# Attention's values in halves of TensorE's columns, in plain float32, in a kernel of attention and MLP

## The chip, the cores and the metric

The kernel runs on one core of a Trainium2 chip. The metric is the device time of one execution in microseconds; a run's time is compared as the median of several executions. The profile is one profiled execution of the same program.

TensorE (PE) multiplies; its weight loads (PEld) are listed apart. VectorE (DVE), ScalarE (ACT) and GpSimd (POOL) work on tiles, and SyncE (SP) issues the loads and stores.

## What is computed

Eight sequences of 576 positions go through banded causal attention with 8 heads of 64, and the result through an MLP with a rational function between its two matrices:

```python
scores = scale * q @ k.T            # per head, scale = 1/8
mask = (rel >= 0) & (rel < 128)     # rel = query position - key position
attn = softmax(where(mask, scores - slope[h] * abs(rel), -1e9))
x = (attn @ v)                      # heads side by side: 4608 x 512
h = x @ w_in                        # 512 x 2048
g = (a0 + a1*h + a2*h**2 + a3*h**3) / (1 + |b0|*|h| + |b1|*h**2 + 1e-6)
out = g @ w_out                     # 2048 x 512
```

All of it is float32.

## The kernel before

**Blocks, tiles and stages.** The 4608 positions are 36 blocks of 128. With a band of 128 a block of queries needs two blocks of keys: its own, below the diagonal, and the one before, above it. The MLP goes through 17 tiles: the first and the last of 3 blocks (384 columns), the others of 2. A unit of attention is a tile of one or two blocks of queries for one pair of heads (4 pairs, 128 rows: 64 of each head). `TILES` lists the units' blocks, `MLP` the tiles' blocks. While the MLP runs on tile t, attention prepares tile t + 1, and in the first stage (t = 0) the weights are converted from 64-bit numbers as well; in the next they are split into high and low parts.

**Number formats.** In the first stage all matmuls take plain float32. In the later ones an operand is split into a high part in the format fp32r (a copy by ScalarE) and the low rest (a subtraction by VectorE), and a product is three matmuls: high x high, low x high, high x low. So `x_hi`, `x_lo`, `wi_hi`, `w_lo`, `g_h`, `g_l` come in twos, as do keys and queries (`kq_hi`, `kq_lo`).

**A unit's way.** `job(u)` loads keys, queries and V (`kqv_raw`), and splits them. The scores (line 433) run with the two heads in the two halves of TensorE's rows, two heads' matmuls for each product. Then VectorE joins and adds the bias (447, 453), ScalarE takes exponentials (458), GpSimd divides by the sum (468), TensorE transposes the probabilities (477, `pt`), ScalarE copies them (480, `p_all`) and VectorE takes their low part (482). GpSimd masks them twice: `p_own` for the own block (488) and `p_all` for the block before (489), each over both parts. The values (500) multiply one block of V, 128 keys by 128 columns of both heads, with the probabilities of both heads side by side, 256 columns, in three matmuls. Of the result `px` half is used: rows of head 0 in head 0's columns, rows of head 1 in head 1's. So two copies (516) and two subtractions (518), of 64 rows each, make `x_hi` and `x_lo`. A unit of two blocks has four such operations, fewer where a sequence begins, and each is placed in TensorE's queue by itself.

**MLP.** Line 599 multiplies x with `w_in` into `h`, lines 622 to 640 compute the rational function, line 655 multiplies with `w_out` into `acc`.

**What sets the order.** Every step is an operation of a plan, with a due time, the engines that can do it and a cost in nanoseconds. Before the program is built the planner goes through time, and gives each free engine the ready operation that is due first. What comes out is a fixed order for each engine's queue. The numbers in capitals (`A0` to `BL`) set the due times. The buffers are rings: `ptx` is one PSUM bank that `pt` and `px` take in turn; `raw` is one buffer.

Of the kernel before, what the change touches and what calls it, by code (L numbers as in the profile page):

```python
# [252 lines left out]
def banded_attention_ratio_mlp(ctx: ExitStack, tc: tile.TileContext, kqv, w_in, w_out, ab, bias, ident, out):  # L253
# [20 lines left out]

# [79 lines left out]
    def job(u):  # L354

        t, p, j = units[u]
        nb = TILES[j]
# [4 lines left out]
        src = kqv[o : o + P * W].rearrange("(q w) -> q w", q=P)
        if t == 0 and j == 0:
            plan.op(u0 - JL, {"s": 364}, lambda e: eng[e].dma_start(ap(first_kq)[:, p], src[:, P : 3 * P]), writes=[(first_kq, p)])
            plan.op(u0 - JL + VL, {"s": 182}, lambda e: eng[e].dma_start(ap(first_v)[:, p], src[:, 4 * P :]), writes=[(first_v, p)])
            kt = lambda part, b0, b1: ap(first_kq)[:, p, (b0 - 1) * P : (b1 - 1) * P]
            qt = lambda part, i: ap(first_kq)[:, p, P : 2 * P]
            vt = lambda part, b: ap(first_v)[:, p]
            return kt, qt, vt, 1, [(first_kq, p)], [(first_v, p)]
        if t == 0:  # L370
            tag = "hi" if p % 2 == 0 else "lo"
            kq = slot(sb2, [P, KMAX + QMAX], F32, "kq_32", tag="kq_" + tag)
            v = slot(sb2, [P, KMAX], F32, "v_32", tag="v_" + tag)
# [11 lines left out]
        plan.op(u0 - JL, {"s": 2002 * W / 1408}, lambda e: eng[e].dma_start(ap(raw)[:, :W], src), writes=[(raw, 0), (raw, 1)], after=1000 * (u0 - AW))  # L385
        for n, (c0, c1) in enumerate(((0, W - ks), (W - ks, W))):
            hi, lo = (kq_hi, kq_lo) if n == 0 else (v_hi, v_lo)
            N = c1 - c0
            plan.op(u0 - 4 + 2 * n, {"a": act(N, 0)}, lambda e, hi=hi, N=N, c0=c0, c1=c1: nc.scalar.copy(ap(hi)[:, :N], ap(raw)[:, c0:c1]), reads=[(raw, n)], writes=[(hi, 0)])
            plan.op(u0 - 3 + 2 * n, {"v": dve(N)}, lambda e, hi=hi, lo=lo, N=N, c0=c0, c1=c1: nc.vector.tensor_tensor(ap(lo)[:, :N], ap(raw)[:, c0:c1], ap(hi)[:, :N].bitcast(F32), ALU.subtract),  # L390
                    reads=[(raw, n), (hi, 0)], writes=[(lo, 0)], sb=True)
# [8 lines left out]
    def attention(u):  # L400
# [67 lines left out]
        plan.op(A + 1.2, {"g": 185 + 1.6 * P * n}, lambda e: nc.gpsimd.tensor_tensor(ap(pr)[:, :n], ap(pr)[:, :n], ap(st)[:, 12 : 12 + n, None].to_broadcast([P, n, P]), ALU.mult),  # L468
                reads=[(pr, y) for y in range(n)] + [(st, 12)], writes=[(pr, y) for y in range(n)])

        pt = slot(ps1, [P, 4 * P], F32, "pt", tag="ptx")
        dt = F32R if parts == 2 else F32
        w = slot(sb2, [P, parts, 4 * P], dt, "p_all")

        def transpose(e):
            for y in range(n):
                nc.tensor.transpose(ap(pt)[:, y * P : (y + 1) * P], ap(pr)[:, y, :], ap(id_sb)[:, 0])  # L477
# [2 lines left out]
        plan.op(A + D2 + 0.2, {"a": act(n * P, 1)}, lambda e: nc.scalar.copy(ap(w)[:, 0, : n * P], ap(pt)[:, : n * P]), reads=[(pt, 0)], writes=[(w, 0)])  # L480
        if parts == 2:
            plan.op(A + D2 + 0.3, {"v": dve(n * P)}, lambda e: nc.vector.tensor_sub(ap(w)[:, 1, : n * P], ap(pt)[:, : n * P], ap(w)[:, 0, : n * P].bitcast(F32)), reads=[(pt, 0), (w, 0)], writes=[(w, 1)])  # L482
        own = w
        if blocks:
            own = slot(const, [P, parts, 4 * P], dt, "p_own")
            pick = lambda y: ap(y)[:, :, : n * P].rearrange("p a (y q) -> p a y q", q=P)
            cost = {"g": 135 + 0.93 * parts * n * P}
            plan.op(A + D2 + 0.5, cost, lambda e: nc.gpsimd.affine_select(out=pick(own), in_=pick(w), pattern=[[0, parts], [0, n], [1, P]], compare_op=ALU.is_ge, fill=0.0, base=0, channel_multiplier=-1), reads=[(w, 0), (w, 1)], writes=[(own, 0), (own, 1)])  # L488
            plan.op(A + D2 + 0.6, cost, lambda e: nc.gpsimd.affine_select(out=pick(w), in_=pick(w), pattern=[[0, parts], [0, n], [-1, P]], compare_op=ALU.is_ge, fill=0.0, base=-1, channel_multiplier=1), reads=[(w, 0), (w, 1)], writes=[(w, 0), (w, 1)])
        if t not in xs:  # L490
            xs[t] = [slot(sb2, [P, NKC, P * MLP[t]], F32 if t == 0 else F32R, "x_hi"), slot(const, [P, NKC, P * MLP[t]], F32R, "x_lo", tag=f"x_lo{t % 2}") if t else None]
        xh, xl = xs[t]
        px = slot(ps3, [P, 4 * P], F32, "px", tag="h") if t == 0 else slot(ps1, [P, 4 * P], F32, "px", tag="ptx")

        def values(e, i, half, first, last):
            y = own if half else w
            c = slice(2 * i * P, 2 * (i + 1) * P)
            seq = ((0, 0), (0, 1), (1, 0)) if parts == 2 else ((0, 0),)
            for k, (a, b) in enumerate(seq):
                nc.tensor.matmul(ap(px)[:, c], vt(a, i + half), ap(y)[:, b, c], start=(first and k == 0), stop=(last and k == len(seq) - 1))  # L500

        for i in range(m):
            halves = [1] if kinds[i] == 1 else [1, 0]
            for k, half in enumerate(halves):
                o3 = plan.op(A + D3, {"p": 357 if parts == 2 else 430}, lambda e, i=i, half=half, k=k, halves=halves: values(e, i, half, k == 0, k == len(halves) - 1),
                        reads=v_keys + [(own if half else w, 0), (own if half else w, 1)], writes=[(px, 0)])
# [4 lines left out]
        b0 = (STARTS[j] - MSTART[t]) * P
        for h in range(2):
            r, dst = slice(64 * h, 64 * h + 64), slice(b0, b0 + m * P)
            src = lambda h=h, r=r: ap(px)[r].rearrange("q (i h c) -> q i h c", i=2, h=2)[:, :m, h]
            into = lambda x, r=r, dst=dst: ap(x)[r, p, dst].rearrange("q (i c) -> q i c", i=m)
            plan.op(A + D3 + 0.3, {"a": act(m * P, 1)}, lambda e, src=src, into=into: nc.scalar.copy(into(xh), src()), reads=[(px, 0)], writes=[(xh, (p, j, h))])
            if t:
                plan.op(A + D3 + 0.4, {"v": dve(m * P)}, lambda e, src=src, into=into: nc.vector.tensor_sub(into(xl), src(), into(xh).bitcast(F32)),
                        reads=[(px, 0), (xh, (p, j, h))], writes=[(xl, (p, j, h))], follows=[raws[k] for k in range(16, 2 * NFC, 2)] if t == 2 else ())
# [239 lines left out]
```

## Time and profile before

| | |
|---|---|
| median of 3 runs | 1083.75 us (1083.62 to 1083.78) |
| profiled execution, its own time | 1083.98 us |
| its span, first to last instruction | 1082.2 us |
| mean granted TensorE clock | 0.997 |

A span is the time from the first to the last instruction; the rest of the execution lies around it. Busy time counts an instruction from its start to its end. TensorE's matmuls are pipelined, so that their ends overlap the next ones' starts, and what one costs in a full queue is read from start to start. A group's row has the line, engine, operation, what is written and read, shapes, count; busy us and mean ns; idle time of the engine before them and what ended it. A row of the timeline has the start and duration in us; x2 are two records merged. In the chain that ended last each moment of the span goes to what the end was waiting for.

### The profile page before, as it was taken

Reading aid. Unit: us, or ns where it says so; the run is one execution under the profiler, and the core shown is the slowest. Engines: PE = TensorE matmul, PEld = TensorE weight load, DVE = VectorE, ACT = ScalarE, POOL = GpSimd, SP = SyncE. Lnnn points to the kernel's source line nnn. Section 1 sums busy time; section 2 is a strip of 40 time slices with the busy share of each in tenths; the row PEclk is TensorE's granted clock in tenths of the full one; section 3 lists DMA queues with packets and bytes.
Section 4 is the critical chain, followed back from the end, with each engine's and each line's share of the span. In section 5 each row is a group of like instructions: output and inputs, shape, how many; then the busy total and the mean of one; then the engine's idle time right before and its main releaser. Section 6 shows DMA issues by size and latency. Waiting matters only on the chain.

```text
span 1082.2 us, 19767 instructions
## 1 busy us (share of the span) xinstructions
PE 1053.0 (97%) x6827; PEld 902.0 (83%) x6827; DVE 948.6 (88%) x2190; ACT 774.1 (72%) x1786; POOL 589.3 (54%) x581
## 2 busy tenths in 40 slices
PE   6899899999999999999999999999999999999998
PEld 4555468899889898989899989989899989888897
DVE  5899899998989898989988889989898989899776
ACT  6766778776767686867776777777676767677664
POOL 3745489854555464546455545555454545546442
PEclk9999999999999999999999999999999999999999
DMA  9625511020201111111111020111110202011000
GB/s 306 202 76 164 151 61 40 26 78 25 79 25 63 46 65 44 60 43 65 42 37 62 28 82 28 63 39 60 44 65 20 80 30 76 21 59 39 20 1 30
DMA packets 35477, 68.79 MB, mean 64 GB/s; under 512 B 3376, under 2 KB 19632, under 8 KB 35376
## 3 DMA queue, kind: packets, MB, share of 16 engines
q1 hardware_dynamic: 35376, 67.52, 19.1%
q8 instruction: 54, 0.88, 0.3%
q14 instruction: 47, 0.39, 0.1%
HBM read 58.07 MB, written 9.44 MB: 62 GB/s over the span
## 4 chain that ended last, share of the span: by engine, by line
PE 82%; DVE 7%; POOL 3%; ACT 3%; DMA 2%; issue 2%; SPq 0%; DVEq 0%; ACTq 0%; POOLq 0%
PE h L599 34%; PE acc L655 33%; PE px L500 8%; PE sc L433 5%; PE pt L477 2%; DMA raw_w<-in_w_out 1%; POOL pr L468 1%; DVE h L632 1%; POOL w_lo L574 1%; DVE g_p L626 1%; ACT pr L458 1%; DVE cv L558 1%; DVE g_p L627 1%; DVE v_lo L390 1%; DVE w L559 1%
## 5 line engine op out<-in xcount | busy, mean ns | idle before, releaser
L599 PE MATMUL h<-x_hi,wi_hi 128*128 128x256 f32 (+1 forms) x1024 | 302.5, 295 | 1.2 <-DVE g_l L640 1.2
L599 PE MATMUL h<-x_lo,wi_hi 128*128 128x256 f32 (+1 forms) x1024 | 291.0, 284 | 0.0
L623 POOL TENSOR_SCALAR g_q<-g_u,babs 128x512 f32<-128x512 f32 (+1 forms) x152 | 116.3, 765 | 307.6 <-ACT g_u L622 292.5
L599 PE MATMUL h<-x_hi,w_lo 128*128 128x256 f32 (+1 forms) x960 | 274.0, 285 | 1.5 <-DVE w_lo L574 1.5
L599 PEld LDWEIGHTS h<-x_lo,wi_hi 128*128 128x128 f32 x1024 | 192.5, 188 | 31.9 <-issue 0.7
L599 PEld LDWEIGHTS h<-x_hi,wi_hi 128*128 128x128 f32 x1024 | 192.6, 188 | 28.2 <-DVE g_l L640 1.8
L655 PE MATMUL acc<-wo_hi,g_h 128*128 128x512 f32 x528 | 209.0, 396 | 0.0
L625 POOL TENSOR_TENSOR g_q<-g_q,g_u 128x512 f32<-128x512 f32 (+1 forms) x152 | 191.0, 1257 | 8.9
L655 PE MATMUL acc<-w_lo,g_h 128*128 128x512 f32 x495 | 194.7, 393 | 0.0
L655 PE MATMUL acc<-wo_hi,g_l 128*128 128x512 f32 x528 | 194.3, 394 | 0.3 <-DVE g_l L640 0.3
L599 PEld LDWEIGHTS h<-x_hi,w_lo 128*128 128x128 f32 x960 | 180.6, 188 | 2.4 <-DVE w_lo L574 1.7
L622 ACT ACTIVATE g_u<-h 128x512 f32<-128x512 f32 (+1 forms) x152 | 87.0, 572 | 101.5 <-PE h L599 99.5
L628 ACT ACTIVATE g_u<-g_q,guard 128x512 f32<-128x512 f32 (+1 forms) x152 | 106.5, 701 | 50.3 <-POOL g_q L625 49.5
L488 POOL TENSOR_SCALAR_AFFINE_SELECT p_own<-p_all 128x1024 fp32r<-128x1024 f32 (+1 forms) x72 | 78.1, 1085 | 89.3 <-DVE p_all L482 88.7
L626 DVE TENSOR_TENSOR g_p<-h,g_p 128x512 f32<-128x512 f32 (+1 forms) x152 | 100.3, 660 | 29.9 <-ACT g_p L624 28.4
L458 ACT ACTIVATE pr<-pr,st 128x128 f32<-128x128 f32 x288 | 112.6, 392 | 18.2 <-DVE st L453 17.4
L631 DVE SCALAR_TENSOR_TENSOR g_q<-g_q,h 128x512 f32<-128x512 f32 (+1 forms) x152 | 99.6, 655 | 29.1 <-ACT h L630 25.4
L624 ACT ACTIVATE g_p<-h,na 128x512 f32<-128x512 f32 (+1 forms) x152 | 114.6, 754 | 0.5 <-DVE h L632 0.2
L640 DVE TENSOR_TENSOR g_l<-h,g_h 128x512 fp32r<-128x512 f32 (+1 forms) x136 | 90.9, 669 | 24.3 <-ACT g_h L639 23.4
L632 DVE SCALAR_TENSOR_TENSOR h<-g_p,na,h 128x512 f32<-128x512 f32 (+1 forms) x152 | 109.5, 720 | 0.1
L627 DVE SCALAR_TENSOR_TENSOR g_p<-g_p,na,h 128x512 f32<-128x512 f32 (+1 forms) x152 | 108.2, 712 | 0.6
L639 ACT CAST g_h<-h 128x512 fp32r<-128x512 f32 (+1 forms) x136 | 77.8, 572 | 40.7 <-DVE h L638 40.3
(91 smaller groups left out, 2257.5 us busy)
## 6 DMA issues: line engine op xcount, KB each, us to landing
kqv_raw<-in_kqv SPq DMA_DIRECT2D x64, 512.0 KB, 3.4
out<-o SPq DMA_DIRECT2D x33, 256.0 KB, 2.4
raw_w<-in_w_in SPq DMA_DIRECT2D x16, 512.0 KB, 4.4
raw_w<-in_w_out SPq DMA_DIRECT2D x16, 512.0 KB, 4.7
bias_t<-in_bias SPq DMA_DIRECT2D x44, 64.0 KB, 1.8
kq<-in_kqv SPq DMA_DIRECT2D x4, 320.0 KB, 5.6
kqv_raw<-in_kqv SPq DMA_DIRECT2D x4, 320.0 KB, 3.5
v<-in_kqv SPq DMA_DIRECT2D x4, 192.0 KB, 5.9
```

Of the source, the lines that this page charges most:

```text
L458: nc.scalar.activation(ap(pr)[:, y, :], ap(pr)[:, y, :], AF.Exp, bias=ap(st)[:, y : y + 1], scale=-1.0, accum_out=ap(st)[:, 4 + y : 5 + y])
L599: nc.tensor.matmul(h(n), w[:, k, :], x[:, k, :], start=(k == 0 and m == 0), stop=(k == NKC - 1 and m == len(seq) - 1))
L623: plan.op(E, {"g": tsc}, lambda e: nc.gpsimd.tensor_scalar(v(g_q), v(g_u), ap(babs)[:, 1:2], ap(babs)[:, 0:1], ALU.mult, ALU.add), reads=[ ...
L624: plan.op(E, {"a": act(W, 1, 2) - 20}, lambda e: nc.scalar.activation(v(g_p), v(h_s), AF.Identity, bias=ap(na)[:, 2:3], scale=ap(na)[:, 3: ...
L625: plan.op(E, {"g": ttc}, lambda e: nc.gpsimd.tensor_tensor(v(g_q), v(g_q), v(g_u), ALU.mult), reads=[(g_q, 0), (g_u, 0)], writes=[(g_q, 0)])
L626: plan.op(E, {"v": dve(W)}, lambda e: nc.vector.tensor_tensor(v(g_p), v(h_s), v(g_p), ALU.mult), reads=[(h_s, 0), (g_p, 0)], writes=[(g_p, ...
L627: plan.op(E, {"v": dve(W, 1)}, lambda e: stt(v(g_p), v(g_p), ap(na)[:, 1:2], v(h_s), ALU.add, ALU.mult), reads=[(h_s, 0), (g_p, 0)], write ...
L628: plan.op(E, {"a": act(W, 0, 1)}, lambda e: nc.scalar.activation(v(g_u), v(g_q), AF.Ln, bias=guard, scale=1.0), reads=[(g_q, 0)], writes=[ ...
L631: plan.op(E, {"v": dve(W)}, lambda e: stt(v(g_q), v(g_q), GUARD, v(h_s), ALU.add, ALU.mult), reads=[(g_q, 0), (h_s, 0)], writes=[(g_q, 0)])
L632: plan.op(E, {"v": dve(W, 1)}, lambda e: stt(v(h_s), v(g_p), ap(na)[:, 0:1], v(h_s), ALU.add, ALU.mult), reads=[(g_p, 0), (h_s, 0)], write ...
L640: plan.op(E, {"v": dve(W)}, lambda e: nc.vector.tensor_tensor(v(g_l), v(h_s), v(g_h).bitcast(F32), ALU.subtract), reads=[(h_s, 0), (g_h, 0 ...
L655: nc.tensor.matmul(ap(accs[t][i]), x[:, sl], w, start=(c == 0 and part == 0 and m == 0), stop=(c == NFC - 1 and (part == 1 or t == 0) and ...
```

## The change

The values run in plain float32 instead of three products of parts. V and the probabilities are then not split: `v_hi`, `v_lo` and the low part of `p_all` are gone, and V is loaded by itself into a tile `v` of three buffers, while keys and queries come in `kq_raw`. The probabilities of the two heads are kept apart, `w[:, h]`, with room for own block and block before in turn, so that the own part of one block of queries and the before part of the next, which need the same block of V, are neighbours. The masks work on half as many elements.

A matmul takes one head's 64 columns of a block of V as weights and writes 64 rows of `px`. `tile_position=(0, 64 * h)` puts head 0 in the left and head 1 in the right half of the array's columns. One block of V serves two blocks of queries at once (256 columns) where both need it, else one (128). All of a unit's values are one operation, placed in the queue in one piece. `px` is then fully used, and one copy and one subtraction of 128 rows make `x_hi` and `x_lo`. The due times' numbers and some costs differ too, so the order of all queues is another.

```diff
-        v_hi = slot(sb2, [P, KMAX], F32R, "v_hi")
-        v_lo = slot(sb2, [P, KMAX], F32R, "v_lo")
-        raw = slot(const, [P, WMAX], F32, "kqv_raw", tag="raw")
+        v = slot(sb3, [P, KMAX], F32, "v")
+        raw = slot(const, [P, KMAX + QMAX], F32, "kq_raw", tag="raw")
...
+        plan.op(u0 - JL, {"s": 2002 * N / 1408}, lambda e: eng[e].dma_start(ap(raw)[:, :N], src[:, :N]), writes=[(raw, 0)], after=1000 * (u0 - AW))
+        plan.op(u0 - JL + VL, {"s": 2002 * ks / 1408}, lambda e: eng[e].dma_start(ap(v)[:, :ks], src[:, N:]), writes=[(v, 0)], after=1000 * (u0 - AW))
...
-        if parts == 2:
-            plan.op(A + D2 + 0.3, {"v": dve(n * P)}, lambda e: nc.vector.tensor_sub(ap(w)[:, 1, : n * P], ap(pt)[:, : n * P], ap(w)[:, 0, : n * P].bitcast(F32)), ...)
...
+            for k, sign in ((1, 1), (0, -1)):
+                plan.op(A + D2 + 0.6 - 0.1 * k, cost, lambda e, k=k, sign=sign: nc.gpsimd.affine_select(out=side(k), in_=side(0), ...), reads=[(w, 0)], writes=[(w, k)])
...
-            for k, (a, b) in enumerate(seq):
-                nc.tensor.matmul(ap(px)[:, c], vt(a, i + half), ap(y)[:, b, c], start=(first and k == 0), stop=(last and k == len(seq) - 1))
+        def values(e):
+            for n, (b, i0, i1) in enumerate(runs):
...
+                for h in range(2):
+                    r = slice(64 * h, 64 * h + 64)
+                    nc.tensor.matmul(ap(px)[r, i0:i1], vt(b)[:, r], ap(w)[:, h, c0 : c0 + i1 - i0], start=new, stop=done, tile_position=(0, 64 * h))
...
-        for h in range(2):
-            r, dst = slice(64 * h, 64 * h + 64), slice(b0, b0 + m * P)
...
+        src = lambda: ap(px)[:, :m].rearrange("q i c -> q (i c)")
+        plan.op(A + D3 + 0.3, {"a": act(m * P, 1)}, lambda e: nc.scalar.copy(into(xh), src()), ...)
```

TensorE's queue before, in the middle of the kernel, from one unit's second values operation on (`px` values, `h` and `acc` the MLP; lines as in the kernel before):

```order
L500 MATMUL px<-p_all,v_hi 128x256 x2
L500 MATMUL px<-p_all,v_lo 128x256
L599 MATMUL h<-x_hi,wi_hi 128x256
L599 MATMUL h<-x_lo,wi_hi 128x256
L599 MATMUL h<-x_hi,w_lo_1564 128x256
L500 MATMUL px<-p_own,v_hi 128x256 x2
L500 MATMUL px<-p_own,v_lo 128x256
```

The three matmuls of an operation stand alone between the MLP's. The same queue now, at such a unit's values (line 509 is the new values line, 603 the former 599, 659 the former 655):

```order
L603 MATMUL h<-x_hi,wi_hi 128x256
L603 MATMUL h<-x_lo,wi_hi 128x256
L603 MATMUL h<-x_hi,w_lo_1457 128x256
L509 MATMUL px<-p_all,v 64x256 x2
L509 MATMUL px<-p_all,v 64x128 x4
L603 MATMUL h<-x_hi,wi_hi 128x256
L603 MATMUL h<-x_lo,wi_hi 128x256
```

Six matmuls, one piece, now carry what twelve in four pieces did. VectorE's queue before, in the first stage, between two units (`cv` and `w` convert weights, `g` belongs to the MLP):

```order
L482 TENSOR_TENSOR p_all<-pt,p_all 128x512
L558 SCALAR_TENSOR_TENSOR cv<-raw_w_345,cv 128x512
L558 SCALAR_TENSOR_TENSOR cv<-raw_w_291,cv 128x512
L390 TENSOR_TENSOR kq_lo<-kqv_raw,kq_hi 128x640
L559 SCALAR_TENSOR_TENSOR w_4_512<-raw_w_291,cv 128x512
L390 TENSOR_TENSOR v_lo<-kqv_raw,v_hi 128x384
L559 SCALAR_TENSOR_TENSOR w_2_380<-raw_w_345,cv 128x512
L626 TENSOR_TENSOR g_p<-h,g_p 128x384
L627 SCALAR_TENSOR_TENSOR g_p<-g_p,na,h 128x384
L390 TENSOR_TENSOR kq_lo<-kqv_raw,kq_hi 128x640
L518 TENSOR_TENSOR x_lo<-px,x_hi 64x256 x2
```

And now, at a unit's keys and another's x in the same stage (387 is the former 390, 522 the former 518, 635, 636, 630 the former 631, 632, 626):

```order
L387 TENSOR_TENSOR kq_lo<-kq_raw,kq_hi 128x640
L463 TENSOR_TENSOR st<-st,tiny 128x4
L464 RECIPROCAL st<-st 128x4
L635 SCALAR_TENSOR_TENSOR g_q<-g_q,h 128x384
L636 SCALAR_TENSOR_TENSOR h<-g_p,na,h 128x384
L630 TENSOR_TENSOR g_p<-h,g_p 128x384
L522 TENSOR_TENSOR x_lo<-px,x_hi 128x256
```

The subtractions for `p_all` and `v_lo` have left the queue, and one for x stands where two did.

More of the change, by code (lines that the diff above doesn't have):

```diff
@@ L367, in job @@
             qt = lambda part, i: ap(first_kq)[:, p, P : 2 * P]
[L368 removed]
+            vt = lambda b: ap(first_v)[:, p]
             return kt, qt, vt, 1, [(first_kq, p)], [(first_v, p)]
         if t == 0:
[L371 to L373 removed]
+            kq = slot(sb2, [P, KMAX + QMAX], F32, "kq_32", tag="kq_hi" if p % 2 == 0 else "kq_lo")
+            v = slot(sb3, [P, KMAX], F32, "v")
             plan.op(u0 - JL, {"s": 728 * 5 / 4}, lambda e: eng[e].dma_start(ap(kq), src[:, : W - ks]), writes=[(kq, 0)])
@@ L381, in job @@
         kq_lo = slot(sb2, [P, KMAX + QMAX], F32R, "kq_lo")
-        v_hi = slot(sb2, [P, KMAX], F32R, "v_hi")
-        v_lo = slot(sb2, [P, KMAX], F32R, "v_lo")
-        raw = slot(const, [P, WMAX], F32, "kqv_raw", tag="raw")
[L385 to L391, printed above, removed]
+        v = slot(sb3, [P, KMAX], F32, "v")
+        raw = slot(const, [P, KMAX + QMAX], F32, "kq_raw", tag="raw")
+        N = W - ks
+        plan.op(u0 - JL, {"s": 2002 * N / 1408}, lambda e: eng[e].dma_start(ap(raw)[:, :N], src[:, :N]), writes=[(raw, 0)], after=1000 * (u0 - AW))
+        plan.op(u0 - JL + VL, {"s": 2002 * ks / 1408}, lambda e: eng[e].dma_start(ap(v)[:, :ks], src[:, N:]), writes=[(v, 0)], after=1000 * (u0 - AW))
+        plan.op(u0 - 4, {"a": act(N, 0)}, lambda e: nc.scalar.copy(ap(kq_hi)[:, :N], ap(raw)[:, :N]), reads=[(raw, 0)], writes=[(kq_hi, 0)])
+        plan.op(u0 - 3, {"v": dve(N)}, lambda e: nc.vector.tensor_tensor(ap(kq_lo)[:, :N], ap(raw)[:, :N], ap(kq_hi)[:, :N].bitcast(F32), ALU.subtract),
+                reads=[(raw, 0), (kq_hi, 0)], writes=[(kq_lo, 0)], sb=True)
         kt = lambda part, b0, b1: ap((kq_hi, kq_lo)[part])[:, b0 * P : b1 * P]
         qt = lambda part, i: ap((kq_hi, kq_lo)[part])[:, ks + i * P : ks + (i + 1) * P]
-        vt = lambda part, b: ap((v_hi, v_lo)[part])[:, b * P : (b + 1) * P]
-        return kt, qt, vt, 2, [(kq_hi, 0), (kq_lo, 0)], [(v_hi, 0), (v_lo, 0)]
+        vt = lambda b: ap(v)[:, b * P : (b + 1) * P]
+        return kt, qt, vt, 2, [(kq_hi, 0), (kq_lo, 0)], [(v, 0)]
     xs = {}
@@ L437, in all_scores @@
                 scores(e, i)
-        o1 = plan.op(A, {"p": 187 + 354 * m if parts == 2 else sum(430 if x else 860 for x in own_only)}, all_scores, reads=kq_keys, writes=[(sc[0], 0), (sc[1], 0)], rows=0.5)
+        o1 = plan.op(A, {"p": 187 + 354 * m if parts == 2 else 187 + sum(215 if x else 430 for x in own_only)}, all_scores, reads=kq_keys, writes=[(sc[0], 0), (sc[1], 0)], rows=0.5)
         blocks = [i for i in range(m) if kinds[i] != 1]
@@ L471, in attention @@
         pt = slot(ps1, [P, 4 * P], F32, "pt", tag="ptx")
-        dt = F32R if parts == 2 else F32
-        w = slot(sb2, [P, parts, 4 * P], dt, "p_all")
+        w = slot(sb2, [P, 2, 4, P], F32, "p_all")
+        base = 0 if blocks else 1
         def transpose(e):
-            for y in range(n):
-                nc.tensor.transpose(ap(pt)[:, y * P : (y + 1) * P], ap(pr)[:, y, :], ap(id_sb)[:, 0])
+            for h in range(2):
+                for i in range(m):
+                    nc.tensor.transpose(ap(pt)[:, (m * h + i) * P : (m * h + i + 1) * P], ap(pr)[:, 2 * i + h, :], ap(id_sb)[:, 0])
@@ L483, in attention @@
-        own = w
+        plan.op(A + D2 + 0.2, {"a": act(n * P, 1)}, lambda e: nc.scalar.copy(side(base), ap(pt)[:, : n * P].rearrange("q (h i c) -> q h i c", h=2, i=m)), reads=[(pt, 0)], writes=[(w, base)])
         if blocks:
[L485 to L489, printed above, removed]
+            cost = {"g": 135 + 0.93 * n * P}
+            for k, sign in ((1, 1), (0, -1)):
+                plan.op(A + D2 + 0.6 - 0.1 * k, cost, lambda e, k=k, sign=sign: nc.gpsimd.affine_select(out=side(k), in_=side(0), pattern=[[0, 2], [0, m], [sign, P]], compare_op=ALU.is_ge, fill=0.0, base=k - 1, channel_multiplier=-sign), reads=[(w, 0)], writes=[(w, k)])
@@ L490, in attention @@
         if t not in xs:
-            xs[t] = [slot(sb2, [P, NKC, P * MLP[t]], F32 if t == 0 else F32R, "x_hi"), slot(const, [P, NKC, P * MLP[t]], F32R, "x_lo", tag=f"x_lo{t % 2}") if t else None]
+            xs[t] = [slot(const, [P, NKC, P * MLP[t]], F32 if t == 0 else F32R, "x_hi", tag=f"x_hi{t % 2}"), slot(const, [P, NKC, P * MLP[t]], F32R, "x_lo", tag=f"x_lo{t % 2}") if t else None]
+        px = slot(ps3, [P, 2, P], F32, "px", tag="h") if t == 0 else slot(ps1, [P, 2, P], F32, "px", tag="ptx")
@@ L502, in attention @@
[L502 to L506, printed above, removed]
+        runs = []
+        for b in range(m + 1):
+            ends = [i for i, half in ((b - 1, 1), (b, 0)) if 0 <= i < m and (half or kinds[i] != 1)]
+            if ends:
+                runs.append((b, ends[0], ends[-1] + 1))
@@ new lines, in attention @@
+        runs.sort(key=lambda r: r[1] - r[2])
+        full = runs[0][2] - runs[0][1] == m
+        if not full:
+            runs.sort()
+        def values(e):
+            for n, (b, i0, i1) in enumerate(runs):
+                new = n == 0 if full else n == 0 or i0 >= runs[n - 1][2]
+                done = n == len(runs) - 1 or not full and runs[n + 1][1] >= i1
+                c0 = 2 * b - 1 if i0 == b - 1 else 2 * b
+                for h in range(2):
+                    r = slice(64 * h, 64 * h + 64)
+                    nc.tensor.matmul(ap(px)[r, i0:i1], vt(b)[:, r], ap(w)[:, h, c0 : c0 + i1 - i0], start=new, stop=done, tile_position=(0, 64 * h))
@@ L507, in attention @@
+        o3 = plan.op(A + D3, {"p": 187 + sum(215 * (i1 - i0) for b, i0, i1 in runs)}, values, reads=v_keys + [(w, 0), (w, 1)], writes=[(px, 0)], rows=0.5)
         stage[u] = (o1, o2, o3)
@@ L511, in attention @@
         b0 = (STARTS[j] - MSTART[t]) * P
-        for h in range(2):
-            r, dst = slice(64 * h, 64 * h + 64), slice(b0, b0 + m * P)
[L514 to L519, printed above, removed]
+        dst = slice(b0, b0 + m * P)
+        src = lambda: ap(px)[:, :m].rearrange("q i c -> q (i c)")
+        into = lambda x: ap(x)[:, p, dst]
+        plan.op(A + D3 + 0.3, {"a": act(m * P, 1)}, lambda e: nc.scalar.copy(into(xh), src()), reads=[(px, 0)], writes=[(xh, (p, j))])
+        if t:
+            plan.op(A + D3 + 0.4, {"v": dve(m * P)}, lambda e: nc.vector.tensor_sub(into(xl), src(), into(xh).bitcast(F32)),
+                    reads=[(px, 0), (xh, (p, j))], writes=[(xl, (p, j))], follows=[raws[k] for k in range(16, 2 * NFC, 2)] if t == 2 else ())
     def x_keys(t, ks, js=None):
-        return [(x, (k, j, h)) for x in xs[t] if x for k in ks for j in range(len(TILES)) if MSTART[t] <= STARTS[j] < MSTART[t] + MLP[t] and (js is None or j in js) for h in range(2)]
+        return [(x, (k, j)) for x in xs[t] if x for k in ks for j in range(len(TILES)) if MSTART[t] <= STARTS[j] < MSTART[t] + MLP[t] and (js is None or j in js)]
     wi_hi = slot(const, [P, NKC, FF], F32R, "wi_hi")
```

24 lines of the change are left out of this document (9 added, 15 removed).

## The prediction

> **What bounds the kernel now.** I read the page first (busy shares and the chain), then busy time by stretch, then the rows around the edit.
>
> ```profile
> span 1082.2 us, 19767 instructions
> PE 1053.0 (97%) x6827; PEld 902.0 (83%) x6827; DVE 948.6 (88%) x2190; ACT 774.1 (72%) x1786; POOL 589.3 (54%) x581
> PE 82%; DVE 7%; POOL 3%; ACT 3%; DMA 2%; issue 2%; SPq 0%; DVEq 0%; ACTq 0%; POOLq 0%
> PE h L599 34%; PE acc L655 33%; PE px L500 8%; PE sc L433 5%; PE pt L477 2%; DMA raw_w<-in_w_out 1%; POOL pr L468 1%; DVE h L632 1%; POOL w_lo L574 1%; DVE g_p L626 1%; ACT pr L458 1%; DVE cv L558 1%; DVE g_p L627 1%; DVE v_lo L390 1%; DVE w L559 1%
> ```
>
> TensorE carries 82% of the chain that ended last, and the values (px, line 500) are 8% of it, 87 us. The stretches show where that share is firm (columns: stretch, its length, then busy us and instructions of each engine, clock, DMA):
>
> ```profile
> 0.00:42.00 42.00, 31.74 (x164) 20.35 (x164) 26.30 (x107) 29.76 (x97) 22.58 (x35) 0.96 0.87 286
> 42.00:115.00 73.00, 67.77 (x243) 37.12 (x242) 65.77 (x148) 48.92 (x106) 39.32 (x48) 0.98 0.40 128
> 115.00:240.00 125.00, 116.89 (x709) 92.20 (x709) 118.60 (x252) 97.70 (x221) 93.58 (x83) 1.00 0.20 64
> 240.00:1015.00 775.00, 773.64 (x5407) 696.55 (x5406) 689.13 (x1593) 559.36 (x1287) 410.32 (x390) 1.00 0.15 49
> 1015.00:1083.00 68.00, 62.99 (x310) 55.81 (x308) 48.84 (x94) 38.34 (x78) 23.51 (x28) 1.00 0.06 20
> ```
>
> From 240 to 1015 us TensorE idles 1.4 us of 775: there a microsecond taken from its queue is a microsecond of the span, and what VectorE, ScalarE and GpSimd save is worth nothing. From 42 to 240 us it idles 5.2 + 8.1 = 13.3 us, while VectorE is busy 184.4 of 198 us; there relief of the others can count. The 10.3 us before 42 us are the start, with its loads and first softmaxes.
>
> **The values on TensorE: what goes.** One old values operation is three matmuls, and it stands in the queue among the MLP's:
>
> ```profile
> 504.07 0.39 PE L500 MATMUL px<-p_own,v_hi 128*128 128x256 f32 x2
> 504.30 0.28 PE L500 MATMUL px<-p_own,v_lo 128*128 128x256 f32 x1
> 504.42 0.28 PE L599 MATMUL h<-x_hi,wi_hi 128*128 128x256 f32 x1
> ...
> L500 PE MATMUL px<-p_own,v_hi 128*128 128x256 f32 x264 | 56.0, 293 | 2.0 <-DVE st L466 1.2 <-POOL p_own L488 0.8
> L500 PE MATMUL px<-p_all,v_hi 128*128 128x256 f32 x240 | 51.7, 297 | 0.7 <-POOL p_all L489 0.6
> ```
>
> Start to start it takes 504.42 - 504.07 = 0.35 us (a matmul's own 0.28 to 0.39 us overlaps the next). Each operation has two v_hi matmuls, so there are (264 + 240) / 2 = 252 of them in the units after the first stage: 252 x 0.35 = 88.2 us, which agrees with the chain's 8%.
>
> **What comes instead.** Per operation the two heads' 128 columns run in plain float32, one head in each half of the array's columns. No row shows column halves. The nearest are the first stage's scores, which run in plain float32 with one head in each half of the rows, and its values on the full array:
>
> ```profile
> 34.88 0.59 PE L500 MATMUL px<-p_own,v 128*128 128x256 f32 x2
> 35.31 0.59 PE L500 MATMUL px<-p_all,v 128*128 128x256 f32 x2
> ...
> 14.16 0.60 PE L500 MATMUL px<-p_all,v_first 128*128 128x256 f32 x2
> 14.68 1.13 PE L433 MATMUL sc<-kq 64*128 64x256 f32 x8
> 15.75 0.70 PE L500 MATMUL px<-p_all,v_first 128*128 128x256 f32 x2
> ```
>
> A plain float32 matmul of 256 columns appears as two records and takes 35.31 - 34.88 = 0.43 us, 0.215 a record. The score block has eight records, four for each head: one after the other they would need 1.72 us, side by side 0.86. From 14.68 to 15.75 it took 1.07, and it began 14.68 - 14.16 = 0.52 after a matmul of 0.43. So row halves do run side by side, and the block costs 0.86 plus 0.09 + 0.21 = 0.30 us for going into the halves and out. I take the same for column halves, as it is the same data type, the same pairing and the same two switches: 0.215 us an operation and 0.30 a unit. There are 64 units of two blocks of queries and 4 of one after the first stage, each now one undivided block: 252 x 0.215 + 68 x 0.30 = 54.2 + 20.4 = 74.6 us. TensorE saves 88.2 - 74.6 = 13.6 us. The ends for the unknown: with the switch hidden, 34.0 us saved, which I hold unlikely, since each score block pays it; with no overlap of the halves, 40.6 lost (a rival below).
>
> "TensorE: Matmul & The Clock Gate" of the Trainium skill (Part 3: Packing small matmuls — row/col tiling) gives three column tiles a speedup of 2.38, that is 0.79 of full overlap. By that figure the 54.2 us would be an estimated 68, TensorE would save nothing, and the sum would be 1075; no column tile runs here, and the row halves above lost nothing but the switch.
>
> **What goes on the other engines.** Rows of one shape each (count, busy us, mean ns):
>
> ```profile
> L390 DVE TENSOR_TENSOR v_lo<-kqv_raw,v_hi 128x384 fp32r<-128x384 f32 x64 | 42.3, 661 | 0.7
> L482 DVE TENSOR_TENSOR p_all<-pt,p_all 128x512 fp32r<-128x512 f32 x64 | 43.8, 684 | 2.3 <-ACT p_all L480 2.2
> L518 DVE TENSOR_TENSOR x_lo<-px,x_hi 64x256 fp32r<-64x256 f32 x128 | 53.8, 420 | 6.9 <-ACT x_hi L516 5.4
> L389 ACT CAST v_hi<-kqv_raw 128x384 fp32r<-128x384 f32 x64 | 32.8, 513 | 1.9 <-PE px L500 0.7
> L516 ACT CAST x_hi<-px 64x256 fp32r<-64x256 f32 x128 | 46.8, 366 | 17.3 <-PE px L500 14.7 <-DVE x_lo L518 1.3
> L488 POOL TENSOR_SCALAR_AFFINE_SELECT p_own<-p_all 128x1024 fp32r<-128x1024 f32 x64 | 73.0, 1141 | 78.4 <-DVE p_all L482 78.2
> L489 POOL TENSOR_SCALAR_AFFINE_SELECT p_all<-p_all 128x1024 fp32r<-128x1024 f32 x64 | 75.0, 1173 | 3.8
> L488 POOL TENSOR_SCALAR_AFFINE_SELECT p_own<-p_all 128x512 f32<-128x512 f32 x4 | 2.5, 636 | 0.3 <-PE px L500 0.3
> ```
>
> A unit saves VectorE 0.66 + 0.68 + 0.42 = 1.77 us (V's low part, the probabilities' low part, one of two subtractions of x), ScalarE 0.51 + 0.37 = 0.88, GpSimd 1.14 + 1.17 - 2 x 0.64 = 1.04. After 240 us that is worth nothing. Before, the chain leads through just these, among the weights' conversion:
>
> ```profile
> 96.35 4.46 DMA raw_w<-in_w_out
> 155.41 1.55 POOL p_own L488
> 158.20 1.63 POOL p_all L489
> 166.00 1.55 DVE v_lo L390
> ...
> 42.00:115.00 73.00, 2.06 (x3) 0.98 0.40 128
> 115.00:240.00 125.00, 4.76 (x7) 1.00 0.20 64
> ```
>
> The last two rows count line 482 alone: ten units between 42 and 240 us. So VectorE loses about 18 of its 184.4 us: 84% of the stretch, less than the 89% (689 of 775) at which it hardly holds TensorE up later. That would take most of the 13.3 us away; but the chain also waits for weights there (4.46 us at 96.35), which the change doesn't touch. I take 8 of the 13.3; ends 0 and 13.3, and above that what idle time doesn't show, since waits shorter than a matmul's overlapping tail leave none.
>
> The first stage's values: four units of two blocks go from four operations of 0.43 to 1.16 us a unit, 2.2 us less in all, four of one block from 0.43 to 0.215 + 0.30, 0.3 more. TensorE waits there; I count 1 us.
>
> **Costed at nothing.** SyncE issues 68 more loads, since V is no longer part of the load of keys and queries; the DMA share after 42 us is 0.15 to 0.40, and V has three buffers and is due after the keys. If that cover went, a late V would hold the whole values block, and behind it the MLP's matmuls. The joined block also waits for both masks at once, where the first operation used to need one only:
>
> ```profile
> PEld px L500 <- POOL p_all L489: 1.8, 8, 0.2
> ```
>
> That is the wait for the masks between 240 and 1015 us: eight times, 0.2 us at most. With 1.04 us less of GpSimd work ahead of it, and some 20 MLP rows between the transposes and the values in the new order, I leave it at nothing.
>
> **Sum.** Against the profiled execution, whose own time is 1083.98 us (span 1082.2, 1.8 around it; the median of the runs is 0.2 lower): 1083.98 - 13.6 - 8 - 1 = 1061.4, forecast 1061 us.
>
> **Rivals.**
>
> *Weight loads come into the open (slower).* Each of the two records of a matmul has its own load. If a half's load can't run under the matmul in flight, it is exposed at every record. Its price is what the scores pay at their first pair:
>
> ```profile
> 500.91 0.39 PE L433 MATMUL sc<-kq_hi 64*128 64x256 f32 x2
> 501.13 0.28 PE L433 MATMUL sc<-kq_lo,kq_hi 64*128 64x256 f32 x2
> 501.25 0.28 PE L433 MATMUL sc<-kq_hi,kq_lo 64*128 64x256 f32 x2
> ```
>
> 0.22 against 0.12 us, so 0.10 exposed. The new order has 192 pairs of matmuls after the first stage, 60 of 256 columns and 132 of 128, so 384 pairs of records, of which 68 open a block and have it in the 0.30 already: 316 x 0.10 = 31.6 us. TensorE would then need 18.0 us more than now, and with 5 us of relief early the time is 1097. It decides against the change from (13.6 + 9) / 316 = 0.07 us a record. Against it: the later pairs of row halves show nothing exposed (0.12), nor do loads on the full array, which last longer than the step from matmul to matmul (0.12 us from 504.30 to 504.42):
>
> ```profile
> L500 PEld LDWEIGHTS px<-p_own,v_hi 128*128 128x128 f32 x264 | 43.5, 188 | 8.7 <-POOL p_own L488 3.6 <-issue 1.4
> ```
>
> Chance 0.07. The same page and part of the Trainium skill say that a weight load overlaps a running matmul only where the row groups differ, which for column halves they don't. On the full array this trace disagrees: loads of 188 ns there run under matmuls of the same rows.
>
> *The halves take turns, so the change doesn't do what it says.* Then 252 x 0.43 + 20.4 = 128.8 us, 40.6 more than before, and 1120 us with 5 of relief. Against it: the row halves. Chance 0.05.
>
> *No relief early.* The stretch to 240 us is held by the weights' loads and their conversion alone: 1083.98 - 13.6 = 1070. For it: the 4.46 us above. Chance 0.20.
>
> *More relief.* All 13.3 us go, and some 8 of waits hidden under matmul tails: 1048. For it: VectorE's 93% there. Chance 0.14.
>
> *A new wait for the joined block.* All 68 units wait as long as the longest wait above, 0.2 us: 13.6 us, and TensorE's gain after the start is gone: 1075. Chance 0.04.
>
> **How the numbers follow.** The forecast's case, 1055 to 1066, has the remaining 0.50. The range 1049 to 1076 takes in the case without relief and most of that with more, and leaves out the two slow rivals (0.12) and some 0.06 below. Faster by over 0.2% (2.2 us, about what a measurement tells from no change) are all but the two slow ones, less a little for a partly exposed load: 0.87; within 0.2% 0.02; slower 0.11.
>
> **What would show it.** Right: the two heads' px matmuls start within some 0.01 us of each other; a values block of 256 + 2 x 128 columns lasts about 1.07 us to the next start; TensorE idle after 240 us stays near 1.4 us and under 8 from 42 to 240; VectorE's busy time falls by about 113 us (64 x 1.77). Wrong: px records of one unit 0.2 us apart with the heads in turn; gaps of 0.3 us inside a block; waits of px for p_all or for V in every unit; or a granted clock below 1.00 after 115 us.

## The result and the profile after

The changed kernel takes 1064.32 us (median of 4 runs, 1063.68 to 1064.7), the kernel before beside it 1083.68 us: 19.4 us faster, a ratio of 0.9823 with a 95% interval of 0.9806 to 0.984. The forecast was 1061 us, its range 1049 to 1076.

The page of the changed kernel, span, busy shares and chain:

```profile
span 1062.6 us, 19670 instructions
PE 1037.1 (98%) x6863; PEld 861.3 (81%) x6863; DVE 834.6 (79%) x1989; ACT 707.4 (67%) x1642; POOL 520.4 (49%) x578
PE 85%; DVE 4%; DMA 4%; POOL 3%; ACT 2%; issue 1%; SPq 0%; DVEq 0%; POOLq 0%; ACTq 0%
```

TensorE bounds it even more, and VectorE has lost 114 us of work. The same stretches as before (PE, PEld, DVE, ACT, POOL, clock, DMA, GB/s):

```profile
0.00:42.00 42.00, 31.34 (x175) 18.82 (x176) 25.46 (x106) 25.06 (x85) 21.66 (x34) 0.80 0.89 297
42.00:115.00 73.00, 68.94 (x268) 36.61 (x267) 61.45 (x138) 46.91 (x101) 36.70 (x49) 0.98 0.41 129
115.00:240.00 125.00, 118.36 (x741) 91.44 (x740) 110.59 (x239) 93.76 (x212) 87.19 (x83) 1.00 0.22 68
240.00:1015.00 775.00, 775.00 (x5473) 676.04 (x5472) 604.63 (x1448) 516.49 (x1194) 359.51 (x396) 1.00 0.15 48
```

From 240 to 1015 us TensorE idles no longer at all; from 42 to 240 it still idles 4.1 + 6.6 = 10.7 us, and before 42 us the clock is lower. One unit's values in TensorE's timeline (start, duration):

```profile
567.18 0.28 PE L603 MATMUL h<-x_hi,w_lo 128*128 128x256 f32 x1
567.39 1.09 PE L509 MATMUL px<-p_all,v 128*64 128x256 f32 x12
568.41 0.73 PE L659 MATMUL acc<-wo_hi,g_l 128*128 128x512 f32 x2
568.98 0.28 PE L603 MATMUL h<-x_hi,wi_hi 128*128 128x256 f32 x1
```

Twelve records in one block, 568.41 - 567.39 = 1.02 us to the next start, begun 0.21 instead of 0.12 after the MLP's last matmul. The single records of that block show the halves side by side; here are their starts in us and columns, two at a time 0.006 to 0.007 us apart:

```
567.390 256   567.397 256
567.657 256   567.664 256
567.873 128   567.879 128
567.982 128   567.989 128
568.091 128   568.098 128
568.200 128   568.207 128
```

How fast the full stretch goes on is read from ScalarE's copies of the finished output, a pair for each tile. The fourth and the fourteenth tile's pair, of the kernel before:

```profile
339.61 1.07 ACT L683 COPY o<-acc 128x512 f32<-128x512 f32 x2
...
905.58 1.07 ACT L683 COPY o<-acc 128x512 f32<-128x512 f32 x2
```

and of the changed kernel:

```profile
331.64 1.09 ACT L687 COPY o<-acc 128x512 f32<-128x512 f32 x2
...
888.94 1.09 ACT L687 COPY o<-acc 128x512 f32<-128x512 f32 x2
```

Ten tiles, which are 40 units, take 566.0 and 557.3 us: 8.7 us less, 0.22 us a unit. Up to the fourth tile's end 8.0 us are gained, behind the fourteenth 1082.2 - 905.6 against 1062.6 - 888.9, so 2.9 us.

### The profile page after: what moved, and what is told of

Read it like the earlier page. It is cut to its first block, busy times and chain, and to the rows that moved or that the text cites. A ratio compares the mean times of both kernels' runs of the same rounds, so it can differ in the third digit from the quotient of the medians.

```text
span 1062.6 us, 19670 instructions
## 1 busy us (share of the span) xinstructions
PE 1037.1 (98%) x6863; PEld 861.3 (81%) x6863; DVE 834.6 (79%) x1989; ACT 707.4 (67%) x1642; POOL 520.4 (49%) x578
## 4 chain that ended last, share of the span: by engine, by line
PE 85%; DVE 4%; DMA 4%; POOL 3%; ACT 2%; issue 1%; SPq 0%; DVEq 0%; POOLq 0%; ACTq 0%
PE h L603 36%; PE acc L659 35%; PE px L509 6%; PE sc L430 5%; PE pt L476 2%; DMA raw_w<-in_w_in 2%; POOL w_lo L578 1%; DMA raw_w<-in_w_out 1%; DVE w L563 1%; DMA kq_raw<-in_kqv 1%; POOL p_all L484 1%; POOL g_q L629 0%; ACT pr L455 0%; DVE cv L562 0%; DVE g_p L630 0%
## 5 line engine op out<-in xcount | busy, mean ns | idle before, releaser
L603 PE MATMUL h<-x_hi,wi_hi 128*128 128x256 f32 (+1 forms) x1024 | 308.2, 301 | 0.0
L629 POOL TENSOR_TENSOR g_q<-g_q,g_u 128x512 f32<-128x512 f32 (+1 forms) x152 | 188.5, 1240 | 9.6
L484 POOL TENSOR_SCALAR_AFFINE_SELECT p_all<-p_all 128x512 f32<-128x512 f32 (+1 forms) x144 | 95.9, 667 | 71.2 <-ACT p_all L480 66.7
L465 POOL TENSOR_TENSOR pr<-pr,st 128x512 f32<-128x512 f32 (+1 forms) x76 | 76.6, 1008 | 84.8 <-DVE st L464 55.3
```

Source lines behind the costliest of these rows:

```text
L484: plan.op(A + D2 + 0.6 - 0.1 * k, cost, lambda e, k=k, sign=sign: nc.gpsimd.affine_select(out=side(k), in_=side(0), pattern=[[0, 2], [0, m ...
L603: nc.tensor.matmul(h(n), w[:, k, :], x[:, k, :], start=(k == 0 and m == 0), stop=(k == NKC - 1 and m == len(seq) - 1))
L629: plan.op(E, {"g": ttc}, lambda e: nc.gpsimd.tensor_tensor(v(g_q), v(g_q), v(g_u), ALU.mult), reads=[(g_q, 0), (g_u, 0)], writes=[(g_q, 0)])
```

## The experiments

Two numbers of each trace are compared: when the fourth tile's first output copy starts (the start-up and the stages with the weights' work lie ahead of it), and how long the next ten tiles take. The first copy of the pair is taken, since the second stands 0.5 us behind it in most of the kernels, but 4.4 us with two units a block and 6.6 with the work given back and old numbers. The marks come from one execution of each kernel; the whole time of a kernel spreads by up to 5.5 us among its executions. Ratios are to the kernel before, run beside each kernel.

| kernel | median us | ratio, 95% interval | fourth tile at us | ten tiles us |
|---|---|---|---|---|
| before | 1083.68 | | 339.6 | 566.0 |
| changed | 1064.32 | 0.9823, 0.9806 to 0.984 | 331.6 | 557.3 |
| changed, old numbers | 1075.57 | 0.9924, 0.9909 to 0.9939 | 342.8 | 558.2 |
| before, new numbers | 1101.13 | 1.0166, 1.0149 to 1.0183 | 355.6 | 566.6 |
| heads in turn | 1088.53 | 1.0048, 1.0033 to 1.0063 | 335.8 | 573.8 |
| all on the full array | 1099.03 | 1.0144, 1.0129 to 1.0159 | 343.3 | 576.8 |
| first stage on the full array | 1067.29 | 0.9849, 0.9834 to 0.9863 | 334.2 | 557.3 |
| work given back, planned | 1095.07 | 1.0109, 1.0094 to 1.0124 | 357.8 | 560.3 |
| work given back, same order | 1122.43 | 1.0361, 1.0346 to 1.0377 | 357.1 | 582.2 |
| work given back, old numbers | 1086.61 | 1.003, 1.0018 to 1.0041 | 351.4 | 557.4 |
| VectorE's and ScalarE's given back | 1078.81 | 0.9962, 0.9947 to 0.9976 | 342.1 | 560.1 |
| GpSimd's given back | 1071.91 | 0.99, 0.9883 to 0.9916 | 336.9 | 558.0 |
| two units a block | 1057.61 | 0.9765, 0.9748 to 0.9782 | 330.8 | 551.0 |
| two units a block, from the second tile | 1066.35 | 0.9848, 0.9827 to 0.9868 | 341.4 | 551.0 |

### Is it the values or the numbers of the plan?

The changed code with the old numbers (`A0` to `BL`), and the old code with the new ones.

```diff
-    A0, DA, T0, L0, L1 = -3.5, 1.542, 22.056, 89.226, 24.76
+    A0, DA, T0, L0, L1 = -3.5, 1.542, 22.056, 90.639, 24.589
...
```

> The changed kernel with the due-time numbers of the kernel before, so that only the code of the change is left. Theory A (the gain is TensorE's shorter values blocks, plus relief of the other engines before 240 us): most of the 19.4 us stays, 1064 to 1072 us. Theory B (the gain is the new order of the queues that the new numbers give): 1078 us or more.

> The kernel before with the due-time numbers of the changed one, its values untouched. Theory A: no gain, 1082 to 1092 us. Theory B: 1065 to 1072 us.

1075.6 us lies between the two expectations, 1101.1 us beyond both. The ten tiles settle it: with the old numbers they take 558.2 us with the new values and 566.0 with the old, with the new numbers 557.3 and 566.6. The numbers act nearly all ahead of the fourth tile: a gain of 11.1 us there for the changed code, and a loss of 16 us for the old code. So theory B falls, but theory A was too simple: of the 19.4 us, 8.3 come with the code alone and 11 with the new numbers. With the old numbers in both, the changed code even reaches the fourth tile 3.1 us later than the kernel before (342.8 against 339.6), though 16 of its shorter blocks and the relief of the other engines lie ahead of it.

### Do the halves overlap, and what by?

First the same matmuls with the heads one after the other in the queue:

```diff
-            for n, (b, i0, i1) in enumerate(runs):
+            for h in range(2):
...
-                for h in range(2):
+                for n, (b, i0, i1) in enumerate(runs):
```

> The changed kernel with all of head 0's values matmuls ahead of all of head 1's in each unit's block, the same matmuls with the same operands. If the halves of the columns overlap because the two heads' matmuls are neighbours in TensorE's queue (theory A), the 252 operations after the first stage go from 0.215 to 0.43 us and the time is some 54 us longer, 1115 to 1120 us, with one record every 0.2 or 0.1 us in a block. If the halves do not overlap at all, or overlap whatever the order, it stays at 1064 us.

It is 24 us slower than the changed kernel, not 54. The timeline of that kernel, one unit:

```profile
569.68 0.28 PE L603 MATMUL h<-x_hi,w_lo 128*128 128x256 f32 x1
569.89 1.57 PE L509 MATMUL px<-p_all,v 128*64 128x256 f32 x12
571.39 0.39 PE L603 MATMUL h<-x_hi,wi_hi 128*128 128x256 f32 x1
571.61 0.28 PE L603 MATMUL h<-x_lo,wi_hi 128*128 128x256 f32 x1
```

The block takes 1.50 us instead of 1.02, not 1.02 + 0.86. Its single records again, starts and columns. The records don't name the head; each head has two of 256 columns and then four of 128, which with their spacing tells the two streams apart:

```
head 0: 569.888 256, 570.155 256, 570.370 128, 570.480 128, 570.589 128, 570.699 128
head 1: 570.376 256, 570.644 256, 570.859 128, 570.968 128, 571.078 128, 571.186 128
```

Head 1's first record starts beside head 0's third, though three of head 0's stand ahead of it in the queue. So the halves do run at once, and matmuls of one half can overtake those of the other, by a few records only: neighbours in the queue overlap wholly, heads in turn by half.

Then plain float32 without halves, the order of the queues kept:

```diff
+                        nc.tensor.matmul(ap(px)[:, 2 * i : 2 * i + 2], vt(i + half), ap(w)[:, :, 2 * i + half], start=k == 0, stop=k == len(halves) - 1)
```

> The changed kernel in the same order and in plain float32, with all values on the full array and both heads' columns, so without the halves; x is again copied in two halves of 64 rows. The 252 operations after the first stage take 0.43 us instead of 0.215 plus the switches (0.30 to 0.36 a unit): 108 against 75 to 78 us on TensorE, 30 to 33 us more: 1094 to 1097 us, slower than the kernel before. If plain float32 and not the halves brought the gain: 1064 to 1070 us.

1099.0 us, 2 beyond the expected range, and 576.8 for ten tiles: 0.49 us a unit more than with halves, and slower than the kernel before. Plain float32 alone is a loss of 15 us; the halves turn it into the gain. On the full array such a block costs nothing beside its matmuls: 1.53 us to the next start and 0.19 more than usual in the MLP's first step after it (0.31 instead of 0.12) make 1.72, which is 4 x 0.43 us.

### What does a block cost beside its matmuls?

Two units' values in one block, from the fourth tile to the last but one:

```diff
+        if paired and p % 2 == 0:
+            pend[u] = todo[0], o1, o2
+            stage[u] = None
+            return
+        if paired:
+            (one, p1, p2) = pend.pop(u - 1)
+            todo = [one] + todo
```

> The changed kernel with the values of two units in one block from the fourth tile to the last but one, so that 26 of the 68 blocks and their switches go; one copy and one subtraction of x for both, and a third buffer for the probabilities. If a block costs 0.30 to 0.36 us beside its matmuls, TensorE saves 8 to 9 us: 1055 to 1057 us. If the switch is hidden or the longer block holds up the MLP's matmuls behind it: 1064 us or more.

1057.6 us, 0.6 beyond the expected end, and better than both kernels: its runs (1055.8 to 1059.65) don't meet the changed kernel's. Its block, of which ten tiles have 20 in place of 40:

```profile
562.94 0.28 PE L621 MATMUL h<-x_hi,w_lo 128*128 128x256 f32 x1
563.15 1.96 PE L511 MATMUL px<-p_all,v 128*64 128x256 f32 x24
565.04 0.39 PE L621 MATMUL h<-x_hi,wi_hi 128*128 128x256 f32 x1
565.26 0.28 PE L621 MATMUL h<-x_lo,wi_hi 128*128 128x256 f32 x1
565.38 0.28 PE L621 MATMUL h<-x_hi,w_lo 128*128 128x256 f32 x1
```

1.89 us for 24 records, against 2 x 1.02, and one entry and one exit less. Ten tiles take 6.3 us less: 0.31 us for each block that went. The exit is seen too: the first MLP step after the block takes 0.22 us, the next 0.12.

The same from the second tile on:

> As the kernel with the values of two units in one block, but from the second tile on, so 4 more blocks and their switches go, 30 in all. By 0.32 us a block, as the full stretch of that kernel shows, 1.3 us less than its 1057.6: 1055 to 1058 us, if the start, where queues have waits, doesn't answer with another order; if it does, 1060 us or more.

Ten tiles take the same 551.0 us, but the fourth tile's mark is at 341.4 instead of 330.8, and the time is 1066.4: where queues wait, another order costs more than the four blocks bring. The expectation named that case.

### What was the relief of the other engines worth?

The work that was taken from VectorE, ScalarE and GpSimd given back, on tiles that nobody reads:

```diff
+        plan.op(u0 - 2, {"a": act(ks, 0)}, lambda e: nc.scalar.copy(ap(x1)[:, :ks], ap(v)[:, :ks]), reads=[(v, 0)], writes=[(x1, 0)])
+        plan.op(u0 - 1, {"v": dve(ks)}, lambda e: nc.vector.tensor_tensor(ap(x1)[:, :ks], ap(v)[:, :ks], ap(x1)[:, :ks].bitcast(F32), ALU.subtract), ...)
...
+            plan.op(A + D2 + 0.3, {"v": dve(n * P)}, lambda e: nc.vector.tensor_sub(ap(x2)..., ap(pt)..., side(base)), reads=[(pt, 0), (w, base)], writes=[(x2, 0)])
...
+                    plan.op(A + D2 + 0.55 - 0.1 * k, cost, lambda e, k=k, sign=sign, x3=x3: nc.gpsimd.affine_select(out=ap(x3)..., in_=side(0), ...), reads=[(w, 0)], writes=[(x3, 0)])
```

> The changed kernel with the work given back to VectorE, ScalarE and GpSimd that the change took from them after the first stage, into tiles that nobody reads: V's copy and subtraction, the probabilities' subtraction, two masks of 512 columns more, x in two halves of 64 rows. TensorE's queue keeps its matmuls. Theory A (relief counts before 240 us only): 1068 to 1073 us, the lost time before 240 us and the stretch from 240 to 1015 us as full as in the changed kernel. Rival (the other engines were half of what held the kernel all along): 1076 us or more, spread over the whole span. Rival (relief was worth nothing): 1064 us.

1095.1 us is beyond theory A's range, but not as its rival has it either: the ten tiles take 560.3 us, 3.0 more than in the changed kernel, while the fourth tile is 26.2 us late. The planner's order differs from the start: the MLP's first matmul comes at 22.65 instead of 20.30 us, before the first given-back instruction (39.6 us). To keep the planner out of it, about the same amount was issued beside existing instructions, in the changed kernel's order:

```diff
-lambda e: nc.vector.tensor_sub(into(xl), src(), into(xh).bitcast(F32))
+lambda e: [nc.vector.tensor_sub(into(xl), src(), into(xh).bitcast(F32)), nc.vector.tensor_sub(idle["v"][:64, :256], idle["s"][:64, :256], idle["s"][:64, :256]), nc.vector.tensor_sub(idle["v"], idle["s"], idle["s"])]
...
```

> The changed kernel with about the work that was taken from the other engines given back to them, on tiles of its own that nothing else reads, and issued beside existing instructions, so that the plan and all queues keep the changed kernel's order (the earlier kernel with given-back work let the planner make another order). Theory A (relief counts before 240 us only): the stretch from 240 to 1015 us moves on at the changed kernel's pace, and some 4 to 9 us are lost before it: 1068 to 1073 us. Rival (other engines hold the kernel everywhere): lost time also after 240 us, 1078 us or more. Rival (relief worth nothing, only the order changed the start): 1064 to 1066 us.

1122.4 us, with the ten tiles at 582.2: here the full stretch suffers too, as the rival has it. TensorE's waits from 240 to 1015 us (who waited for whom, total us, times, longest):

```profile
PE px L511 <- POOL p_all L486: 16.1, 13, 1.6
PE pt L478 <- POOL pr L467: 10.3, 20, 1.3
```

In the changed kernel neither is there. An order that was made for short masks leaves the longer ones no slack; a planner that knows of them finds one that does (560.3). Here each given-back mask stood right ahead of the real one, and VectorE's pieces take 2.02 us a unit where 1.77 were taken away. So this is probably harsher than the old work was; by how much isn't shown.

With the old numbers and the work given back, little of the change but TensorE's part is left:

> The changed kernel with the taken-away work given back to VectorE, ScalarE and GpSimd (planned, as in the first such kernel) and with the due-time numbers of the kernel before: of the change hardly more than TensorE's part is left. Theory A' (TensorE's part is worth some 0.22 us a unit wherever the queue is full, so 10 us between 200 and 850 us, and the start depends on numbers and load): the full stretch moves on 6 to 10 us faster than in the kernel before, and the whole is 1076 to 1090 us depending on the start. Rival (the halves need the relief everywhere): no gain in the full stretch, 1085 to 1095 us.

The full stretch keeps the gain whole, 557.4 us for ten tiles, while the fourth tile's mark is at 351.4, 8.6 us later than with the old numbers alone, and the whole, 1086.6 us, is no gain. So TensorE's part doesn't need the relief where TensorE is full; the start does. It shows in the stretches of that kernel; from 42 to 240 us TensorE was busy 182.23 us with the old numbers alone, and 187.30 in the changed kernel:

```profile
0.00:42.00 42.00, 29.66 (x159) 17.57 (x159) 26.18 (x106) 27.03 (x85) 19.08 (x30) 0.73 0.83 278
42.00:240.00 198.00, 175.00 (x889) 117.16 (x891) 170.62 (x378) 138.89 (x316) 128.75 (x143) 0.95 0.27 88
```

Last, one part of the given-back work at a time: without GpSimd's, and GpSimd's alone.

> The changed kernel with only VectorE's and ScalarE's work given back (V's copy and subtraction, the probabilities' subtraction, x in two halves). Theory D (VectorE is what holds the stretch from 42 to 240 us, at 93% before): most of the 31 us that the whole given-back work cost comes back here, 1080 to 1095 us, lost before 240 us. Rival (the longer masks were it): 1064 to 1072 us.

> The changed kernel with only GpSimd's work given back (two more masks of 512 columns a unit). Theory D: 1064 to 1070 us, since GpSimd has room. Rival (the masks stand in a unit's chain, and GpSimd's splitting of weights waits behind them): 1075 to 1090 us.

VectorE's and ScalarE's share costs 14.5 us, of them 10.5 ahead of the fourth tile; GpSimd's costs 7.6, of them 5.2 there. Theory D has the order right, but both missed their ranges by 1 to 2 us, and the two together make 22 of the 31 us. How the planner orders the start differs in each, so that the sum can't be told apart further.

### Does the clock hold the start?

The first stage's values alone on the full array, by the edit above with `whole = t == 0`.

> The changed kernel with the first stage's values on the full array (128 columns of V, both heads' columns, as in the kernel before), all later units unchanged and the order of the queues the same. Theory C (the halves keep TensorE's clock at half for 20 of the first 55 us, and the first stage starts 2 to 4 us late for that): the clock before 42 us rises from 0.80 towards 0.96 and the time falls to 1061 to 1063 us. Rival (the start waits for loads, softmax and conversion anyway): 1064 to 1066 us whatever the clock.

1067.3 us, 3 us slower than the changed kernel, with the clock before 42 us at 0.76:

```profile
0.00:42.00 42.00, 31.55 (x136) 20.15 (x137) 23.42 (x103) 25.98 (x87) 20.45 (x32) 0.76 0.86 287
```

Theory C falls: the halves don't bring the clock down. What does was not found, and the rival missed its range too, by 1.3 us. Since the clock didn't rise, it also stays open what a full clock would bring.

Past the start the clock and TensorE's waits go together, and no experiment separates the two. In the planned kernel with all work given back, TensorE waited 6.96 us up to 187.00 us; from 185 to 191 us the granted clock was 0.50, and the MLP's steps took 0.21 instead of 0.12 us:

```profile
187.00 0.79 PE L671 MATMUL acc<-wo_hi,g_h 128*128 128x512 f32 x1 [6.96 <-ACT g_h L655]
...
189.09 0.41 PE L615 MATMUL h<-x_lo,wi_hi 128*128 128x256 f32 x1
189.30 0.42 PE L615 MATMUL h<-x_hi,w_lo 128*128 128x256 f32 x1
```

From 42 to 240 us the mean clock was 0.99 in the kernel before and in the changed one, 0.95 in the changed code with old numbers and 0.94 in this kernel. By an estimate from these means, up to 0.05 x 198 = 10 of its 26.2 us can be the clock's, which fell with the waits, and not the waits' alone.

## Why the prediction came out right, and which terms were off

**TensorE's part** was put at 13.6 us, 0.20 a unit. Measured are 0.22 us a unit over 40 units (0.19 with the old numbers in both kernels, 0.23 with the new in both); for all 68, 14.8 us. Its working held, with two errors that nearly cancel: the block lasts 1.02 us, not 1.07, but it also costs the MLP 0.10 us in its first step afterwards, which the prediction didn't count. By the block's parts that is 4 x 0.35 - (1.02 + 0.09 + 0.10) = 0.19 a unit; from joining two blocks came 0.31 for a block's overhead, beside the 0.30 that was taken over from the row halves.

**The relief early** was put at 8 us, and 1 for the first stage's values: this is the term that was mis-sized. 19.4 - 14.8 leaves 4.6 us. TensorE's idle time from 42 to 240 us fell from 13.3 to 10.7 only, and the fourth tile's lead of 8.0 us is 3.5 from its 16 units at 0.22 and 4.5 from the rest. The prediction took VectorE's load for the measure, at which TensorE would be held up little. It fell from 184.4 to 172.0 of 198 us, but the largest of TensorE's waits from 42 to 240 us, the MLP's for VectorE's g (line 635, now 639), is 4.9 us in both kernels: it did not go down with the load. The wait for the masks grew, from 0.8 + 0.6 us to 2.7:

```profile
PE h L599 <- DVE g L635: 4.9, 4, 2.0
...
PE px L500 <- POOL p_own L488: 0.8, 1, 0.8
...
PE px L500 <- POOL p_all L489: 0.6, 2, 0.4
...
PE h L603 <- DVE g L639: 4.9, 5, 1.7
PE px L509 <- POOL p_all L484: 2.7, 2, 1.9
```

The experiments show why one number couldn't do: ahead of the fourth tile the same code gives 342.8 or 331.6 us by the plan's numbers alone, and giving the work back costs 8.6 us there with the old numbers (351.4 against 342.8) and 26.2 with the new. Relief and order together made the 4.6 us; the prediction had only the relief, and no term for the numbers. That its sum came within 3.3 us is in this part luck: the same code with the old numbers, 1075.6 us, was 14.6 us from the forecast and just inside the range. What the lower clock before 42 us (0.80 against 0.96) took from the 4.6 us isn't known.

**Costed at nothing.** V's separate loads and the joined block held nobody up in the full stretch; of waits for the masks one of 0.4 us is left on the weight loads' side from 240 to 1015 us:

```profile
PEld px L509 <- POOL p_all L484: 0.4, 1, 0.4
```

The statement that the other engines' work is worth nothing after 240 us holds for a planned order to 0.1 to 3.0 us in ten tiles (557.4 to 560.3), and not for a fixed one.

**The rivals.** Weight loads in the open and heads in turn did not come: records of 256 columns follow each other in 0.216 us (0.267 for a block's first) and those of 128 in 0.109, with the loads of both halves under them. The rule of the Trainium skill ("TensorE: Matmul & The Clock Gate", Part 3: Packing small matmuls — row/col tiling) that loads overlap only for differing row groups is so not borne out for column halves either. Nor is the 0.79 of full overlap, worked out from its speedup of 2.38 for three narrower tiles: with the heads in turn, one half alone goes at the same pace (0.215 and 0.110 us) as both together. No relief early (1070) and more relief (1048) both were further off than the forecast. Of the marks set, TensorE's idle time from 42 to 240 us (under 8 us) was missed, and the clock before 42 us was not foreseen.

## What to carry to other kernels

Where TensorE's queue is full, price an edit by start-to-start times in that queue, switches into and out of the halves included: 0.3 us a block left 0.2 of some 0.5 us of gain a unit, and putting two units into one block brought the next 7 us. Put the two heads' matmuls next to each other in the queue, since heads in turn gave half of the overlap back. What relief of other engines is worth where TensorE waits depends on the order made for it, and on which waits it reaches: look at each wait's own chain, not at the load alone. Test it apart from the full stretch, with two marks in the trace that stand at the same amount of work in every kernel.

## What the runs showed of the hardware that was not expected

Matmuls in one half of the columns overtook those of the other half that stood ahead of them in the queue, by three records (heads in turn: head 1's first at 570.376, head 0's fourth at 570.480). After a block in halves the MLP's first step took 0.22 us instead of 0.12, beside the 0.09 on entry. A plain float32 matmul of 64 columns had weight loads of 139 ns, against 192 for the 128 columns of the values on the full array, though the transposes' loads of 128 columns took only 143 in the changed kernel:

```profile
L509 PEld LDWEIGHTS px<-p_all,v 128*64 128x64 f32 x816 | 48.7, 139 | 28.1 <-POOL p_all L484 7.0 <-issue 4.3 <-POOL raw_w L560 0.8
```
